# A gated mix of linear attention and a state-space convolution: moving rows by transfers, sums in plain fp32, and a reordered passage

## The chip, the cores and the metric

The kernel runs on one core of a Trainium2 chip. The metric is the device time of one execution in microseconds; lower is better. A core has five engines with a queue each: PE (TensorE, matrix products), DVE (VectorE), ACT (ScalarE), POOL (GpSimd) and SP (SyncE, which issues most transfers). Each takes its instructions in order and waits for the others through semaphores. Products are accumulated in PSUM, a memory of eight banks; all else lies in SBUF, 128 partitions wide.

## The reference

For a sequence of 2048 rows and 448 channels, two branches are mixed by a gate:

```python
g = sigmoid((x * gate_w).sum(-1, keepdims=True))
# A: linear attention, 16 heads of 28
q, k, v = split(x @ wqkv)                # heads of 28 channels
phi = lambda t: where(t > 0, t + 1, exp(t)) + 1e-6
kv  = einsum("bhsd,bhse->bhde", phi(k), v)
z   = phi(k).sum(over s)
o   = einsum("bhqd,bhde->bhqe", phi(q), kv) / (einsum("bhqd,bhd->bhq", phi(q), z) + 1e-6)
a   = o.reshape(B, S, D) @ wo
# B: each channel of x convolved with a long filter made from (log_A, A_imag, C, log_dt), plus x * D_skip
out = g * a + (1 - g) * b
```

With the inputs given here the filter of branch B is so flat that the convolution is the filter's first tap times a running sum of x. The kernel makes sure of that from the parameters (the number `okn`), and has a general convolution behind a branch that these inputs don't take.

## The kernel before

The 2048 rows are 16 pieces (`c` = 0 to 15) of 128. Matrix products are done in two or three steps on `float32r` operands: each operand is split into a high part (a cast on ScalarE) and a low part (a subtraction on VectorE or POOL), and high x high, high x low and low x high are added in PSUM. The order on each engine is the order in which the program is written; there is no scheduler.

**Main loop** (`c` = 2 to 14). Each turn does on PE: `project(c + 1, wkh, wkl, ...)`, eleven products for `k` of the next piece; one or two pairs of `do_v`, the running sum of x (a triangular matrix `tri` times `xn`); `project(c, wqh, wql, ...)`, eleven for `q`; `do_g(c)`, eleven that add phi(k)^T x into the four banks `g`. ScalarE and VectorE make phi(k) (`k_feature`, `k_high`, `k_low`; the last also adds phi(k) into `zb`, the sum of k by partition) and phi(q) (`q_post`, which writes `pq` and the gate's exponentials `e1`). POOL makes the low parts of the next pieces (`split_t`, `split_n`) and adds the running sums into `y` (`v_post`). SP loads three pieces ahead and writes the last row of each piece's running sum into row c of `u`, from which the carry between pieces comes.

`s4d_prepare` is cut into steps by `yield`; `steps(n)` runs n of them. The last computes the first tap by channel: VectorE ends with `sm` (`p0`), PE spreads it over the partitions with four transposes (`p`), and ScalarE copies it to `near`, which `v_post` needs from piece 0 on. In the loop `steps(3 if c == 4 else 1)` stands behind `q_post(c)` and ahead of `do_g(c)`, so the transposes stand between `q` and `g` of piece 4.

**The passage** (from `gate(0, NC - 1)`). The sum of k over partitions (`zo`) is taken by a matrix of ones, with `zb` split into `zh` and `zl`; it returns to `zb` on all partitions. `norm_a` multiplies `pq` by it (`prod`, POOL), `norm_b` and `norm_d` make the denominators (`den`, VectorE), `norm_c` the normalized rows (`pn`: two pieces of it on POOL, a small one on VectorE). The last `do_g` turns fill `g`, ScalarE copies it to `gs`, `kv_products(r)` multiplies it by `wv`, and `kv_split(r, ...)` masks the heads and splits (`kvh`, `kvl`). `inter` makes the carry rows `rc` from `zst`, the rows of `u` split and stacked, and the 0/1 matrix `gcat`. `mrows(j, ...)` multiplies block j of `kv` by block j of `wo`: the output matrix, four blocks of 112 rows, which replaces the weights of `k` (`mh`, `ml` = `wkh`, `wkl`). Block 3 goes to `sh`, `sl`; its rows must be moved to other partitions: 16 of them under each of blocks 0 to 2, 64 into `mh[:, 3]` and `rc`. That is done by products with the 0/1 matrix `pick`: two in each of the first three `mrows`, two in `tails()`.

**The attend loop** (`c` = 0 to 15): `turn(c + 2)` transposes `pn` (`tr`) and splits it (`th`, `tl`), `attend(c)` does eleven products `a` with the output matrix, `final_b` and `final_c` mix and send piece c - 1, `norm_c(c + 3)`, `norm_a(c + 6)`, `norm_b(c + 5)` prepare later pieces. The `q` products of piece 15 are kept as filler: `q_run(n)` does the next n of them.

Buffers matter to the order: `prod` and `pn` have two each, so a third can only be written when the reader of the first has ended.

Of the kernel before, what the change touches and what calls it, by code (L numbers as in the profile page):

```python
# [31 lines left out]
QA = (2, 2, 5)  # L32
# [7 lines left out]
KZ = 32 + NC - 1  # L40
# [129 lines left out]
def gated_mix_kernel(ctx: ExitStack, tc: tile.TileContext, xin, wq_d, wv_d, wo_d, abc_d, ldt_d, dsk_d,  # L170
                     tri_d, ident_d, mask_d, gcat_d, sel_d, pick_d, first_d, nabc_d, nldt_d, xrev_d, lag_d, out):
# [218 lines left out]
    def k_low(c):  # L390
        pk = pks.pop(c)
        pkl[c] = tp.tile([P, D], F32R, name="pkl", tag="pkl")
        for o, a, op in ((pkl[c], pkh[c].bitcast(F32), ALU.subtract), (zb, zb, ALU.add)):
            DVE.scalar_tensor_tensor(out=o, in0=pk, scalar=1e-6, in1=a, op0=ALU.add, op1=op)
# [51 lines left out]

    def z_products():
        zr = tp.tile([P, D], F32, name="zr", tag="w")[:64]
        POOL.memset(zr, 0.0)
        for o in (0, 32):  # L450
            SP.dma_start(out=zr[o:o + NC - 1], in_=u[:NC - 1])
        return zr
# [45 lines left out]
    for c in range(2, NC - 1):  # L498
        if c + 3 < NC:
            load_x(c + 3)  # L500
        if c == 2:
# [13 lines left out]
        if c + 2 < NC:
            split_t(c + 2)
        if c == NC - 2:
            zr = z_products()
            pick = xt_p.tile([P, 5, P], F32R, name="pick", tag="t")[:DJ]
            ACT.copy(pick, pickr)  # L520
# [5 lines left out]
        if c == NC - 2:
            zh = tp.tile([P, D], F32R, name="zh", tag="e")
            zl = tp.tile([P, D], F32R, name="zl", tag="t")
            ACT.copy(zh, zb)
            low(DVE, zl, zb, zh)  # L530
# [9 lines left out]
        if c == 4:  # L540
            steps(1)
            POOL.tensor_copy(gcat, gcr)
        if c + 2 < NC:
            split_n(c + 2)
# [110 lines left out]
    ACT.copy(zst, zr[:KZ])
    low(DVE, zst[32:], zr[32:KZ], zst[32:])
    zo = ps.tile([P, 512], F32, name="k", tag="k")
    do_g(NC - 2, (0, 1, 2))
    PE.matmul(zo[:1, D:D + 1], lhsT=ones[:DJ, :1], rhs=oks, start=True, stop=True)
    PE.matmul(zo[:, :D], lhsT=ones_r, rhs=zh, start=True, stop=False)  # L660
    PE.matmul(zo[:, :D], lhsT=ones_r, rhs=zl, start=False, stop=True)
    ACT.copy(zb, zo[:, :D])
# [4 lines left out]
    norm_bd(0)
    norm_a(2)
    for i in range(4):
        do_g(NC - 1, (i,))  # L670
        ACT.copy(gs[i], g[i][:, :D])
        if i == 2:
            gates_b(g2, "pkl")()
    norm_bd(1)
    norm_a(3)
    norm_c(0)
    norm_c(1)
    norm_bd(2)
    qo, q_run = pieces(NC - 1, wqh, wql, D + 2, "q")
    q_run(QA[0])  # L680
    for c in range(5):
        phi(c)
# [5 lines left out]
    def inter():  # L688
        o = ps.tile([P, 512], F32, name="z", tag="v0")
        r = tp.tile([P, D], F32R, name="rc", tag="w")  # L690
        z = tp.tile([P, D], F32R, name="zs", tag="v0")
# [1 line left out]
        PE.matmul(o[:RX, :D], lhsT=gcat, rhs=zst, start=True, stop=True)
# [4 lines left out]
    def mrows(j, pool, tag):
        o = pool.tile([P, 512], F32, name="m%d" % j, tag=tag)
        if j < 3:  # L700
            for n, w in enumerate((sh, sl)):
                PE.matmul(o[:, :D], lhsT=pick[:, j], rhs=w, start=n == 0, stop=False)
        w = woh[j]
        for n, (a, b) in enumerate(((kvh, w), (kvh, wol[j]), (kvl, w))):
            PE.matmul(o[:DJ, :D], lhsT=a[:, j], rhs=b, start=j == 3 and n == 0, stop=n == 2)  # L705
        if j < 3:
            a, b = mh[:, j], ml[:, j]
        else:
            a, b = sh, sl
        ACT.copy(a, o[:a.shape[0], :D])  # L710
        DVE.tensor_tensor(out=b, in0=o[:a.shape[0], :D], in1=a.bitcast(F32), op=ALU.subtract)

    sh = tp.tile([P, D], F32R, name="sh", tag="v0")[:DJ]
    sl = tp.tile([P, D], F32R, name="sl", tag="pkl")[:DJ]

    def tails():
        o = ps.tile([P, 512], F32, name="md", tag="v1")
        for i, w in ((3, sh), (4, sl)):
            PE.matmul(o[:, :D], lhsT=pick[:, i], rhs=w, start=i == 3, stop=i == 4)
        ACT.copy(mh[:, 3], o[:, :D])  # L720
        ACT.copy(rc[0][:DT], sh[:DT].bitcast(F32))
# [9 lines left out]
    def kv_split(r, kvp):  # L731
        m = 3 if r else 2
        DVE.tensor_tensor(out=kv[:, 2 * r:m],
                          in0=kvp[:DJ, 2 * r * DJ:m * DJ].rearrange("p (j d) -> p j d", d=DJ),
                          in1=mask[:, None, :].to_broadcast([DJ, m - 2 * r, DJ]), op=ALU.mult)
        if r:
            a, b = (w.rearrange("p (h d) -> p h d", h=4) for w in (kvp[:DJ, 3 * DJ:4 * DJ], mask))
            DVE.tensor_tensor(out=kv[:, 3, :DT].rearrange("p (h d) -> p h d", h=4), in0=a[:, :, DS:], in1=b[:, :, DS:],
                              op=ALU.mult)
# [3 lines left out]
        ACT.copy(kvh[:, rs], kv[:, rs])
# [11 lines left out]
    norm_c(2)  # L755
    q_run(QA[2])
    turn(1)
    tails()
    mrows(2, ps, "v0")
    mrows(0, p3, "a")  # L760
    mrows(1, p3, "a")
    norm_a(4)
# [65 lines left out]
def _layout(inputs):  # L828
# [41 lines left out]
    pick = np.zeros((DJ, 5, P))  # L870
    for i in range(DT):
        pick[i, 3, i] = pick[i, 4, DT + i] = 1.0
    for i in range(DJ - DT):
        pick[DT + i, i // 16, DJ + i % 16] = 1.0
# [38 lines left out]
```

## Time and profile before

| | us |
|---|---|
| median of 3 runs | 192.49 |
| the runs | 191.38, 192.49, 193.17 |
| the profiled execution, as timed | 191.0 |
| its span, first to last instruction | 189.1 |
| busy: PE, DVE, ACT, POOL | 175.4, 112.4, 96.3, 119.2 |
| mean granted TensorE clock | 0.984 |

The profile is of one execution. Its chain of waits is the work that ended last, followed back from the end; 78% of it is PE. A row of the timeline gives start, length, engine, line, operation, output and inputs with their sizes, and in brackets how long the engine had stood still and for whom. Rows that follow each other on PE overlap, since products are pipelined: the distance between starts tells what one costs. Times in the text are from the span's start.

### The profile page before, as it was taken

The numbers are of one execution on the slowest core, as the hardware profiler recorded it, in microseconds if no ns is written. First come the engines' busy times: TensorE is split into PE (matmuls) and PEld (weight loads), VectorE is DVE, ScalarE is ACT, GpSimd is POOL, SyncE is SP. The second block draws the span as 40 slices with busy tenths as digits, with TensorE's granted clock in tenths as the row PEclk, the third lists the DMA queues.
The fourth block names the chain that finished last, engine by engine and source line by source line (L and its number), as shares of the span: only waits on it lengthen the run. The fifth ranks groups of instructions, "written<-read, shape, count | busy, mean of one in ns | idle before, by whom it ended". The sixth has DMA issues, their size and how long they took to land.

```text
span 189.1 us, 2750 instructions
## 1 busy us (share of the span) xinstructions
PE 175.4 (93%) x886; PEld 154.3 (82%) x886; DVE 112.4 (59%) x238; ACT 96.3 (51%) x215; POOL 119.2 (63%) x126
## 2 busy tenths in 40 slices
PE   6999999974999999999999999998699999999980
PEld 2697798964899999999989999967599999999970
DVE  1658647745072652734625526489799999987430
ACT  3768289863062462533626644480574545564340
POOL 3359874570629697696788999367557877864000
PEclk9999999999799999999999999999999999999997
DMA  6999958900003023031233020000001212221231
GB/s 192 412 302 277 307 158 304 279 6 0 3 0 111 1 111 112 5 111 25 87 111 115 0 62 0 11 2 4 2 0 49 93 57 98 98 97 51 101 123 38
DMA packets 7771, 18.53 MB, mean 98 GB/s; under 512 B 1755, under 2 KB 4390, under 8 KB 7750
## 3 DMA queue, kind: packets, MB, share of 16 engines
q1 hardware_dynamic: 7750, 18.28, 29.1%
q8 instruction: 9, 0.15, 0.3%
q14 instruction: 12, 0.10, 0.2%
HBM read 14.50 MB, written 3.67 MB: 96 GB/s over the span
## 4 chain that ended last, share of the span: by engine, by line
PE 78%; DVE 6%; ACT 4%; POOL 4%; DMA 3%; issue 2%; SPq 1%; ACTq 0%; POOLq 0%; DVEq 0%
PE a L639 19%; PE g L425 17%; PE k L356 16%; PE q L356 15%; PE tr L617 3%; DMA xr<-in 3%; PE v L433 2%; PE v L432 2%; POOL wql L264 2%; PE m L705 1%; POOL xn L264 1%; PE v L356 1%; DVE den L565 1%; DVE pn L586 1%; POOL y L276 1%
## 5 line engine op out<-in xcount | busy, mean ns | idle before, releaser
L384 DVE SCALAR_TENSOR_TENSOR k<-k,e 128x448 f32<-128x448 f32 x14 | 8.9, 633 | 48.1 <-ACT e L383 48.1
L425 PE MATMUL g<-pkh,xn 128*128 128x448 f32 x112 | 36.4, 374 | 0.3 <-POOL xn L264 0.3
L438 POOL TENSOR_TENSOR y<-y,t 128x448 f32<-128x448 f32 x16 | 18.5, 1154 | 18.2 <-DVE t L437 18.0
L356 PE MATMUL q<-wqh,xt 128*128 128x450 f32 x120 | 28.0, 369 | 0.0
L264 POOL TENSOR_TENSOR xn<-xr,xn 128x448 fp32r<-128x448 f32 x16 | 18.5, 1154 | 14.2 <-ACT xn L274 14.2
L356 PE MATMUL k<-wkh,xt 128*128 128x448 f32 x112 | 27.1, 381 | 0.0
L639 PE MATMUL a<-wkh,th 128*128 128x448 f32 (+1 forms) x119 | 26.9, 365 | 0.0
L356 PEld LDWEIGHTS q<-wqh,xt 128*128 128x128 f32 x120 | 22.5, 189 | 2.1 <-issue 0.2
L425 PEld LDWEIGHTS g<-pkh,xn 128*128 128x128 f32 x112 | 21.4, 191 | 3.4 <-POOL xn L264 0.7
L425 PE MATMUL g<-pkl,xn 128*128 128x448 f32 x64 | 24.0, 375 | 0.0
L356 PEld LDWEIGHTS k<-wkh,xt 128*128 128x128 f32 x112 | 21.6, 194 | 2.7 <-ACT wkh L456 0.4
L382 ACT ACTIVATE e<-k 128x448 f32<-128x448 f32 x14 | 7.6, 545 | 31.7 <-PE k L356 31.7
L560 POOL TENSOR_TENSOR prod<-pq,zb 128x448 f32<-128x448 f32 x16 | 18.4, 1151 | 5.5 <-DVE den L565 4.0
L639 PEld LDWEIGHTS a<-wkh,th 128*128 128x128 f32 x119 | 20.5, 189 | 1.3
L276 POOL TENSOR_TENSOR y<-xr,rows 128x448 f32<-128x448 f32 x16 | 18.4, 1148 | 1.0 <-DMA rows<-in 1.0
L264 POOL TENSOR_TENSOR xt<-xr,xt 128x512 fp32r<-128x512 f32 x14 | 18.1, 1295 | 0.0
L583 POOL TENSOR_TENSOR pn<-pq,den 128x336 f32<-128x336 f32 x16 | 12.1, 754 | 8.9 <-PE tr L617 6.9
L621 ACT CAST th<-tr 128x512 fp32r<-128x512 f32 x16 | 9.4, 588 | 15.8 <-PE tr L617 15.5
L644 DVE SCALAR_TENSOR_TENSOR ot<-y,og,a 128x448 f32<-128x448 f32 (+1 forms) x17 | 10.5, 618 | 6.5 <-PE a L639 6.4
L639 PE MATMUL a<-wkl,th 128*128 128x448 f32 (+1 forms) x51 | 12.6, 356 | 0.0
L388 ACT ACTIVATE pkh<-k 128x448 fp32r<-128x448 f32 x14 | 7.6, 545 | 9.8 <-DVE k L384 9.8
L356 PE MATMUL q<-wql,xt 128*128 128x450 f32 x45 | 12.1, 367 | 0.4 <-POOL wql L264 0.4
(160 smaller groups left out, 338.1 us busy)
## 6 DMA issues: line engine op xcount, KB each, us to landing
xr<-in SPq DMA_DIRECT2D x15, 512.0 KB, 5.8
out<-ot SPq DMA_DIRECT2D x15, 224.0 KB, 1.9
pq<-in SPq DMA_DIRECT2D x4, 448.0 KB, 11.1
y<-in SPq DMA_DIRECT2D x2, 480.0 KB, 4.3
y<-in SPq DMA_DIRECT2D x2, 450.0 KB
wv<-in SPq DMA_DIRECT2D x1, 896.0 KB
wo<-in SPq DMA_DIRECT2D x1, 784.0 KB, 9.1
y<-in SPq DMA_DIRECT2D x1, 448.0 KB
```

The lines of the kernel that those rows point to most:

```text
L264: eng.tensor_tensor(out=o, in0=r, in1=h.bitcast(F32), op=ALU.subtract)
L276: POOL.tensor_tensor(out=y[:, c], in0=r[:, :D], in1=dsk, op=ALU.mult)
L356: PE.matmul(o[:, :n], lhsT=a, rhs=b, start=run.n == 1, stop=not seq)
L382: ACT.activation(e, pks[c], AF.Relu, scale=-1.0)
L384: DVE.scalar_tensor_tensor(out=pks[c], in0=pks[c], scalar=1.0, in1=e, op0=ALU.add, op1=ALU.max)
L425: PE.matmul(g[i][:a.shape[1], :D], lhsT=a, rhs=b, start=c == 0 and n == 0, stop=c == NC - 1 and n == len(seq) - 1)
L438: POOL.tensor_tensor(out=y[:, c], in0=y[:, c], in1=t, op=ALU.add)
L560: POOL.tensor_tensor(out=pd[c], in0=pq[:, c], in1=zb, op=ALU.mult)
L583: POOL.tensor_tensor(out=n[:, :3, :DJ].rearrange("p j (h d) -> p j h d", h=4), in0=a, in1=r[:, :H - 4].rearrange("p (j h) -> p j h", j=3)[ ...
L621: ACT.copy(h, ov)
L639: PE.matmul(a[:, lo:hi], lhsT=u_, rhs=w_[:, lo:hi], start=n == 0, stop=n == 10)
L644: DVE.scalar_tensor_tensor(out=ot[:, lo:hi], in0=y[:, c, lo:hi], scalar=og[:, c:c + 1], in1=a[:, lo:hi], op0=ALU.mult, op1=ALU.add)
```

## The change

Seven edits go together.

- The tap transposes: `steps(2 if c == 4 else 1)` and a `steps(1)` behind `project` of turn 5.
- The main loop ends with `c` = 13. Turn 14 is written out at the head of the passage, with `zo` between `q` and `g` of piece 14, the gate cut in two (pieces 0 to 13, then 14), and POOL's addition of the last running sum (`v_add`) moved to a later place. In `k_low(15)` the sum into `zb` comes first.
- The sum of k: `zb` is multiplied by `ones` as plain fp32; `zh`, `zl` and `ones_r` go.
- The carry: `u` is multiplied by `gcat` as plain fp32; `zst`, `z_products` with its two transfers, and the cast of `gcat` go.
- The rows of block 3: `pick` and its load and cast, its eight products and `tails()` go. `mrows(3)` writes high and low part side by side (`shl`), and four transfers take the rows to their partitions: three issued by SP, one by ACT. Two ScalarE copies of 64 rows do the rest. `wkh` and `wkl` become two halves of one tile `wk2`, so that one transfer serves both.
- `kv_split` is cut: the low part is now `kv_low(r)`, placed apart.
- The passage's order: `inter` ahead of the `kv` products, both of these ahead of the masks, `norm_c(0)` and `norm_c(1)` early, `norm_bd(3)` behind `turn(1)`, ten of the eleven `q` products of piece 15 in one run behind it.

```diff
-QA = (2, 2, 5)
+QA = 1
...
-        for o, a, op in ((pkl[c], pkh[c].bitcast(F32), ALU.subtract), (zb, zb, ALU.add)):
+        for o, a, op in ((pkl[c], pkh[c].bitcast(F32), ALU.subtract), (zb, zb, ALU.add))[::-1 if c == NC - 1 else 1]:
...
+        if c == 5:
+            steps(1)
...
-        steps(3 if c == 4 else 1)
-        if c < NC - 2:
-            do_g(c)
...
+        if c < 5:
+            steps(2 if c == 4 else 1)
+        do_g(c)
...
+    c = NC - 2
+    ko = project(c + 1, wkh, wkl, D, "k")
+    do_v(c + 1)
+    k_feature(c + 1, ko)
+    k_high(c + 1)
+    gate(0, c)
+    k_low(c + 1)
+    vl = v_post(c + 1)
+    qo = project(c, wqh, wql, D + 2, "q")
+    zo = ps.tile([P, 512], F32, name="zo", tag="v0")
+    PE.matmul(zo[:1, D:D + 1], lhsT=ones[:DJ, :1], rhs=oks, start=True, stop=True)
+    PE.matmul(zo[:, :D], lhsT=ones, rhs=zb, start=True, stop=True)
+    q_post(c, qo)
+    ACT.copy(zb, zo[:, :D])
+    norm_a(0)
+    norm_a(1)
+    do_g(c)
+    gate(c, c + 1)
...
+    inter()
+    q_run(QA)
     k1 = kv_products(1)
+    k0 = kv_products(0)
+    norm_bd(2)
+    norm_a(3)
     kv_split(1, k1)
-    k0 = kv_products(0)
+    kv_low(1)
     kv_split(0, k0)
-    inter()
-    q_run(QA[1])
     mrows(3, ps, "k")
+    for j, eng in ((2, SP), (0, ACT), (1, SP)):
+        eng.dma_start(out=wk2[DJ:, :, j].bitcast(F32), in_=shl[DT + 16 * j:DT + 16 * j + 16].bitcast(F32))
+    SP.dma_start(out=mh[DT:, 3].bitcast(F32), in_=shl[:DT, 1].bitcast(F32))
+    kv_low(0)
+    mrows(2, ps, "v0")
     turn(0)
+    v_add(c + 1, vl)
+    norm_c(2)
+    norm_a(4)
+    mrows(0, p3, "a")
+    ACT.copy(mh[:DT, 3], shl[:DT, 0].bitcast(F32))
+    mrows(1, p3, "a")
+    ACT.copy(rc[0][:DT], shl[:DT, 0].bitcast(F32))
+    turn(1)
     norm_bd(3)
...
```

On PE around the taps, before (`p` are the transposes, `q` and `g` those of piece 4):

```order
L356 MATMUL q<-wqh,xt 128x450 x8
L356 MATMUL q<-wql,xt 128x450 x3
L337 MATMUL p<-ident,sm 128x112 x4
L425 MATMUL g_145<-pkh,xn 128x448
L425 MATMUL g_145<-pkl,xn 128x448
```

and in the changed kernel, from the end of `g` of piece 4 (`wk_69` is the joint tile of the weights, `k` that of piece 6):

```order
L422 MATMUL g_144<-pkl,xn 128x448
L422 MATMUL g_144<-pkh,xn 128x448
L422 MATMUL g_145<-pkl,xn 64x448
L422 MATMUL g_145<-pkh,xn 128x448
L353 MATMUL k<-wk_69,xt 128x448 x11
L334 MATMUL p<-ident,sm 128x112 x4
L429 MATMUL v<-xn,tri 128x448
L430 MATMUL v<-xn,tri 128x448
```

The transposes have moved behind twenty-two products.

On ACT in the passage, before, from the cast of `kvh` (`m` is the result of `mrows`, block 3 first; `md` that of `tails`):

```order
L743 CAST kvh<-kv 112x224 x2
L694 CAST zs<-z 48x448
L710 CAST sh<-m_1366 112x448
L621 CAST th<-tr 128x512 x2
L720 CAST wkh<-md 128x448
L721 CAST rc<-sh 64x448
L710 CAST wkh<-m_1405 128x448
L710 CAST wkh<-m_1413 128x448
L710 CAST wkh<-m_1421 128x448
L625 CAST th<-rows 48x128
```

and now:

```order
L709 CAST kvh<-kv 112x224 x2
L686 CAST shl<-m_1342 112x448
L726 DMA wk_69<-shl 16x2x448
L686 CAST wk_69<-m_1353 112x448
L598 CAST th<-tr 128x512
L686 CAST wk_69<-m_1374 112x448
L735 CAST wk_69<-shl 64x448
L686 CAST wk_69<-m_1381 112x448
L737 CAST rc<-shl 64x448
L598 CAST th<-tr 128x512
L602 CAST th<-rows 48x128
```

The issue of a transfer stands among the copies, and the copy of block 2 ahead of the first `th`.

On POOL in the passage, before (`prod` is `norm_a`, `pn` is `norm_c`, `y<-y,t` the last running sum):

```order
L449 MEMSET zr 64x448
L438 TENSOR_TENSOR y<-y,t 128x448
L654 MEMSET rows 48x896
L560 TENSOR_TENSOR prod<-pq,zb 128x448 x4
L583 TENSOR_TENSOR pn<-pq,den 128x3x112
L589 TENSOR_TENSOR pn<-pq,den 128x128
L583 TENSOR_TENSOR pn<-pq,den 128x3x112
L589 TENSOR_TENSOR pn<-pq,den 128x128
L583 TENSOR_TENSOR pn<-pq,den 128x3x112
L589 TENSOR_TENSOR pn<-pq,den 128x128
L560 TENSOR_TENSOR prod<-pq,zb 128x448 x2
```

and now:

```order
L537 TENSOR_TENSOR prod<-pq,zb 128x448 x2
L648 MEMSET rows 48x896
L560 TENSOR_TENSOR pn<-pq,den 128x3x112
L566 TENSOR_TENSOR pn<-pq,den 128x128
L537 TENSOR_TENSOR prod<-pq,zb 128x448
L560 TENSOR_TENSOR pn<-pq,den 128x3x112
L566 TENSOR_TENSOR pn<-pq,den 128x128
L537 TENSOR_TENSOR prod<-pq,zb 128x448
L441 TENSOR_TENSOR y<-y,t 128x448
L560 TENSOR_TENSOR pn<-pq,den 128x3x112
L566 TENSOR_TENSOR pn<-pq,den 128x128
L537 TENSOR_TENSOR prod<-pq,zb 128x448 x2
```

The first two `pn` have moved between the `prod`, and the last running sum behind `prod` of piece 3.

More of the change, by code (lines that the diff above doesn't have):

```diff
@@ L39 @@
 RX = DT + 3 * NC
-KZ = 32 + NC - 1
 FAR = 2.0 ** 100
@@ L170, in gated_mix_kernel @@
 def gated_mix_kernel(ctx: ExitStack, tc: tile.TileContext, xin, wq_d, wv_d, wo_d, abc_d, ldt_d, dsk_d,
-                     tri_d, ident_d, mask_d, gcat_d, sel_d, pick_d, first_d, nabc_d, nldt_d, xrev_d, lag_d, out):
+                     tri_d, ident_d, mask_d, gcat_d, sel_d, first_d, nabc_d, nldt_d, xrev_d, lag_d, out):
     nc = tc.nc
@@ L187, in gated_mix_kernel @@
     const = work.enter_context(tc.tile_pool(name="const", bufs=1))
-    wkh = const.tile([P, J, D], F32R, name="wkh")
-    wkl = const.tile([P, J, D], F32R, name="wkl")
+    wk2 = const.tile([P, 2, J, D], F32R, name="wk2")
+    wkh, wkl = wk2[:, 0], wk2[:, 1]
     wqh = const.tile([P, J, D + 2], F32R, name="wqh")
@@ L196, in gated_mix_kernel @@
     mask = const.tile([DJ, DJ], F32, name="mask")
-    gcat = const.tile([KZ, RX], F32R, name="gcat")
+    gcat = const.tile([NC - 1, RX], F32, name="gcat")
     sel = const.tile([P, 1], F32, name="sel")
-    zst = const.tile([KZ, D], F32R, name="zst")
-    ones_r = const.tile([P, P], F32R, name="ones_r")
     ones = const.tile([P, P], F32, name="ones")
@@ L437, in v_post, with v_add @@
         DVE.tensor_tensor(out=t, in0=vt.pop(c)[:, :D], in1=near, op=ALU.mult)
-        POOL.tensor_tensor(out=y[:, c], in0=y[:, c], in1=t, op=ALU.add)
         if c < NC - 1:
             SP.dma_start(out=u[c:c + 1], in_=t[P - 1:P])
+            v_add(c, t)
+        return t
+    def v_add(c, t):
+        POOL.tensor_tensor(out=y[:, c], in0=y[:, c], in1=t, op=ALU.add)
     prep = s4d_prepare()
@@ L445, in steps @@
             next(prep, None)
[L447 to L452, printed above, removed]
     w = xt[0] = xt_p.tile([P, 2 * NAT], F32R, name="xt", tag="t")
@@ L492, in gated_mix_kernel @@
     DVE.memset(ones, 1.0)
-    DVE.tensor_copy(ones_r, ones)
     q_post(1, qo)
@@ L497, in gated_mix_kernel @@
     woh, wol = [], []
-    for c in range(2, NC - 1):
+    for c in range(2, NC - 2):
         if c + 3 < NC:
@@ L501, in gated_mix_kernel @@
         if c == 2:
-            gcr = tp.tile([P, D], F32, name="gcr", tag="w")[:KZ, :RX]
-            for o, i in ((mask, mask_d), (gcr, gcat_d), (sel, sel_d)):
+            for o, i in ((mask, mask_d), (gcat, gcat_d), (sel, sel_d)):
                 SP.dma_start(out=o, in_=i)
@@ L507, in gated_mix_kernel @@
             SP.dma_start(out=wo, in_=wo_d)
-        if c == NC - 3:
-            pickr = xp.tile([P, 5, P], F32, name="pickr", tag="xr")[:DJ]
-            SP.dma_start(out=pickr, in_=pick_d)
         vs = VS.get(c, ())
         ko = project(c + 1, wkh, wkl, D, "k")
+        if c == 5:
+            steps(1)
         for v in vs[:1]:
             do_v(v)
[L515 to L520, printed above, removed]
+        split_t(c + 2)
         k_feature(c + 1, ko)
@@ L525, in gated_mix_kernel @@
         k_low(c + 1)
[L526 to L530, printed above, removed]
         qo = project(c, wqh, wql, D + 2, "q")
@@ L536, in gated_mix_kernel @@
             v_post(v)
-        steps(3 if c == 4 else 1)
-        if c < NC - 2:
-            do_g(c)
[L540 to L544, printed above, removed]
+        if c < 5:
+            steps(2 if c == 4 else 1)
+        do_g(c)
+        split_n(c + 2)
         for j in {11: (0, 1), 12: (2, 3)}.get(c, ()):
@@ L650, in final_c @@
             ACT.copy(pq[:, c, lo:hi], a[:, lo:hi])
-    gate(0, NC - 1)
+    c = NC - 2
[16 more added lines that the diff above has]
+    gate(c, c + 1)
     g2 = gates_a(1, NC - 1)
     POOL.memset(rows[DT:RX, :2 * D], 0.0)
[L655 to L662, printed above, removed]
+    last = gates_b(g2, "pkl")
     DVE.tensor_copy(okn, zo[:1, D:D + 1])
-    norm_a(0)
-    norm_a(1)
-    do_g(NC - 2, (3,))
     norm_bd(0)
+    norm_c(0)
+    last()
     norm_a(2)
+    norm_bd(1)
+    norm_c(1)
     for i in range(4):
-        do_g(NC - 1, (i,))
+        do_g(c + 1, (i,))
         ACT.copy(gs[i], g[i][:, :D])
[L672 to L682, printed above, removed]
+    qo, q_run = pieces(c + 1, wqh, wql, D + 2, "q")
+    for i in range(5):
+        phi(i)
     gps.close()
@@ L692, in inter @@
         rc.append(r)
-        PE.matmul(o[:RX, :D], lhsT=gcat, rhs=zst, start=True, stop=True)
+        PE.matmul(o[:RX, :D], lhsT=gcat, rhs=u[:NC - 1], start=True, stop=True)
         ACT.copy(z[DT:RX], o[DT:RX, :D])
@@ L696, in inter @@
                                  in1=o[DT:RX, :D], op0=ALU.mult, op1=ALU.add)
+    shl = xn_p.tile([P, NX], F32R, name="shl", tag="n")[:DJ, :2 * D].rearrange("p (i d) -> p i d", i=2)
     def mrows(j, pool, tag):
         o = pool.tile([P, 512], F32, name="m%d" % j, tag=tag)
-        if j < 3:
-            for n, w in enumerate((sh, sl)):
-                PE.matmul(o[:, :D], lhsT=pick[:, j], rhs=w, start=n == 0, stop=False)
         w = woh[j]
         for n, (a, b) in enumerate(((kvh, w), (kvh, wol[j]), (kvl, w))):
[L705 to L721, printed above, removed]
+            PE.matmul(o[:DJ, :D], lhsT=a[:, j], rhs=b, start=n == 0, stop=n == 2)
+        a, b = (mh[:DJ, j], ml[:DJ, j]) if j < 3 else (shl[:, 0], shl[:, 1])
+        ACT.copy(a, o[:DJ, :D])
+        DVE.tensor_tensor(out=b, in0=o[:DJ, :D], in1=a.bitcast(F32), op=ALU.subtract)
     def kv_products(r):
@@ L743, in kv_split, with kv_low @@
         ACT.copy(kvh[:, rs], kv[:, rs])
+    def kv_low(r):
+        rs = slice(2 * r, 2 * r + 2)
         low(DVE, kvl[:, rs], kv[:, rs], kvh[:, rs])
+    inter()
+    q_run(QA)
     k1 = kv_products(1)
+    k0 = kv_products(0)
+    norm_bd(2)
+    norm_a(3)
     kv_split(1, k1)
-    k0 = kv_products(0)
+    kv_low(1)
     kv_split(0, k0)
-    inter()
-    q_run(QA[1])
     mrows(3, ps, "k")
-    turn(0)
-    norm_bd(3)
[L755 to L762, printed above, removed]
+    for j, eng in ((2, SP), (0, ACT), (1, SP)):
[3 more added lines that the diff above has]
+    mrows(2, ps, "v0")
+    turn(0)
+    v_add(c + 1, vl)
[6 more added lines that the diff above has]
+    turn(1)
+    norm_bd(3)
     norm_a(5)
@@ L865, in _layout @@
     k = np.arange(NC)[None, :] - np.arange(NC)[:, None]
-    gcat = np.zeros((KZ, RX))
-    gcat[:NC - 1, DT:] = gcat[32:, DT:] = np.repeat(k[:-1] > 0, 3, axis=1)
+    gcat = np.zeros((NC - 1, RX))
+    gcat[:, DT:] = np.repeat(k[:-1] > 0, 3, axis=1)
     sel = np.zeros((P, 1))
     sel[DT:RX, 0] = -1.0 * (np.arange(RX - DT) % 3 == 1)
[L870 to L874, printed above, removed]
     h = np.arange(DJ) // DH
@@ L889, in _layout @@
         f(sel),
-        f(pick),
         first,
```

## The prediction

> **What bounds the kernel now.** I read the busy shares first, then PE's waits, then the chain of waits. The first fence has PE's row of the busy shares and the longest rows of PE's waits (who waited for whom: us in total, times, longest).
>
> ```profile
> PE 175.4 (93%) x886; PEld 154.3 (82%) x886; DVE 112.4 (59%) x238; ACT 96.3 (51%) x215; POOL 119.2 (63%) x126
> ...
> PE p L337 <- DVE sm L303: 3.7, 1, 3.7
> ...
> PE m L705 <- ACT kvh L743: 1.5, 1, 1.5
> PE k L728 <- ACT gs L671: 0.6, 1, 0.6
> ```
>
> TensorE is the bound, so the change is worth what it takes from PE's work and from PE's waits. The largest wait is one: the tap transposes `p` wait 3.7 us for VectorE. The chain of waits (start us, us, what) shows what surrounds it, the windows below it the granted clock (after the five engines come the clock, then the DMA share and GB/s), and the timeline two operations of ScalarE.
>
> ```profile
> 39.27 0.55 ACT e L382
> 39.85 0.59 ACT e L383
> ...
> 41.70 0.62 DVE pkl L394
> ...
> 44.96 0.17 DVE sm L303
> ...
> 45.18 0.60 PE p L337 x4
> 45.77 3.27 PE g L425 x11
> 49.05 2.76 PE k L356 x11
> 51.81 0.21 PE v L432
> ...
> 54.90 2.27 PE g L425 x11
> 57.16 2.25 PE k L356 x11
> ...
> 40.00:50.00 10.00, 6.30 (x27) 5.28 (x26) 3.97 (x19) 3.04 (x7) 5.29 (x6) 0.83 0.00 1
> 50.00:60.00 10.00, 10.00 (x50) 9.13 (x49) 3.77 (x7) 3.80 (x8) 4.44 (x5) 1.00 0.11 35
> ...
> 45.81 0.53 ACT L338 COPY rows<-p 128x448 f32<-128x448 f32 x1 [3.64 <-PE p L337]
> 46.76 0.62 ACT L268 CAST xt<-xr 128x512 fp32r<-128x512 f32 x1
> ```
>
> The reader is to see two losses. PE stands still from 45.18 - 3.7 = 41.48 to 45.18. Then the same eleven `g` products take 3.27 where they take 2.27 an iteration later, and `k` 2.76 for 2.25: the clock granted over 40 to 50 us is 0.83, and 1.00 in the next window.
>
> **Part 1: the tap transposes one iteration later.** They move behind `g` of piece 4 and `k` of piece 6. Before, 41.48 to 51.81, where the first `v` starts, is 10.33 us. After, the same work is 2.27 (`g`) + 2.25 (`k`) + 0.44 (four transposes, the `tr` row of the next fence) = 4.96. That is a gain of 5.37, of which 1.51 is the clock (3.27 - 2.27 + 2.76 - 2.25).
>
> Is the cover there? `p` would start at 41.48 + 4.52 = 46.0; its input `sm` ends at 44.96 + 0.17 = 45.13 and follows from nothing that PE does after 41.48. Next to be late is `k` of piece 7, due at 46.0 + 0.44 + 2.25 + 2.27 + 0.82 (two `v` pairs) = 51.8. It needs its PSUM bank, and ScalarE now copies the taps ahead of that work: transposes done 46.5, copy 0.53, cast of `xt` 0.62, two exponentials 0.55 and 0.59 = 48.8, then four VectorE passes at about 0.62 (the `pkl` row) = 51.3. Half a microsecond is left, so I charge nothing. SP's queue keeps its order there. The POOL cast of `gcat` and the VectorE cast of `ones_r` go, neither waited for by PE.
>
> **Part 2: PE's work in the passage.** The passage runs from `k` of the last piece to the second `a`. The fence has chain rows, then timeline rows of PE.
>
> ```profile
> 116.71 2.24 PE k L356 x11
> ...
> 123.55 0.41 PE k L660
> 123.95 0.47 PE k L661
> ...
> 134.00 0.90 PE m L705 x3
> ...
> 141.43 2.25 PE a L639 x11
> 143.69 0.44 PE tr L617 x4
> 144.13 2.26 PE a L639 x11
> ...
> 129.79 1.74 PE L728 MATMUL tr<-gs,wv 128*112 128x112 f32 x16
> 131.46 0.46 PE L693 MATMUL z<-zst,gcat 47*112 47x448 f32 x1
> ...
> 137.38 0.36 PE L702 MATMUL m<-sh,pick 112*128 112x448 f32 x1
> ...
> 137.79 0.57 PE L705 MATMUL m<-wo,kvh 112*112 112x448 f32 x2
> ```
>
> The eight `pick` products go: two of them run from 137.38 to 137.79, so 8 x 0.205 = 1.64 us less. The sums become plain fp32. No 448-column fp32 product is in the trace; the nearest are the eight 112-column ones (16 records) from 129.79 to 131.46, 0.209 each, four times that for 448 columns: 0.84. The lower end is the split product's own 0.205, the upper 1.74/8 x 4 = 0.87. I take 0.84: `zo` costs 0.84 for 0.41 + 0.47, `z` 0.84 for 0.46. PE's work falls by 1.64 + 0.04 - 0.38 = 1.30 at face value. Counted out, the new passage up to the second `a` holds 23.4 us of PE work: `k`, `v`, `q` 4.90, `zo` 0.96 with the small product, two `g` and `o` 4.64, `z` 0.84, `q` 2.25, `kv` 3.34, four `m` 2.44, four `tr` 1.76, the first `a` 2.25. Before, the stretch lasted 144.13 - 116.71 = 27.42. So 4.04 us is the most the passage can give.
>
> **Part 3: the waits of the new passage.** I reckon on the old clock, each engine in its new order, with these durations (timeline, the waits' causes in brackets; DMA rows: KB each, us to landing).
>
> ```profile
> 125.33 1.00 DVE L411 TENSOR_SCALAR og<-og 128x15 f32<-128x15 f32 x1
> 128.09 0.62 DVE L565 TENSOR_REDUCE den<-prod 128x16 f32<-128x448 f32 x1
> 132.41 0.47 DVE L570 SCALAR_TENSOR_TENSOR den<-den,e 128x16 f32<-128x16 f32 x1
> 162.44 0.14 DVE L779 TENSOR_SCALAR og<-og 128x1 f32<-128x1 f32 x1
> ...
> 125.14 2.26 POOL L560 TENSOR_TENSOR prod<-pq,zb 128x448 f32<-128x448 f32 x2 [1.55 <-ACT zb L662]
> 132.10 0.75 POOL L583 TENSOR_TENSOR pn<-pq,den 128x336 f32<-128x336 f32 x1
> 132.81 0.40 POOL L589 TENSOR_TENSOR pn<-pq,den 128x128 f32<-128x128 f32 x1
> 161.64 1.15 POOL L560 TENSOR_TENSOR prod<-pq,zb 128x448 f32<-128x448 f32 x1
> ...
> 129.40 3.59 SPq L597 DMA_DIRECT2D rows<-phs  x5
> ...
> out<-ot SPq DMA_DIRECT2D x2, 112.0 KB, 2.1
> pq<-in SPq DMA_DIRECT2D x4, 448.0 KB, 11.1
> ```
>
> VectorE and POOL hinder each other: two small VectorE operations last until a POOL operation ends, L570 until L583 does (132.10 + 0.75 = 132.85, and 132.41 + 0.47 = 132.88), L411 until the first `prod` does (125.14 + 1.13 = 126.27, and 126.33).
>
> - `zo` must wait for the last sum into `zb`, which stands behind the three gate operations: `k` ends at 118.95, two exponentials, one VectorE pass, the gate (0.5) and the pass into `zb` make 122.0, and PE is there at 121.6: 0.4.
> - The old 1.5 before `m` (kvh) shrinks. PE ends the `kv` products at 116.71 + 4.90 + 0.4 + 0.96 + 4.64 + 0.84 + 0.2 + 3.34 = 132.0. VectorE has the denominators of piece 2 just ahead of the masks; their second operation, L570, waits for `prod` 3 on POOL. POOL starts the first `prod` near 123.7, behind `zo` and a copy of 0.53, and runs without a gap through `prod` 0 and 1, a memset, `pn` 0, `prod` 2, `pn` 1 and `prod` 3 to about 131.2. From L570's end to `m` it was 134.00 - 132.88 = 1.1: 132.3. PE waits 0.3. The 0.6 before `kv` is covered by `z` and one `q`.
> - After the first `m` (132.3 to 132.9) ScalarE copies its rows into `shl` behind the second `kvh` cast, 133.9, and VectorE makes their low part, 134.5. Only then comes `kvl` for block 0, whose inputs both lie in SBUF like L570's; it runs into POOL's `pn` 2, which starts after `tr` 0 near 134.1, so it ends at 134.1 + 0.75 + 0.35 (half a pass) = 135.2. PE wants it at 134.35: 0.9.
> - The new wait is at `tr` of piece 3. ScalarE issues one row transfer, and that issue waits for `shl` low at 134.5 with everything behind it waiting too; SP's issues take 3.59/5 = 0.72, so 135.2 (bounds: nothing and 1.4, twice as much). Behind it stand seven ScalarE copies of 0.53 to 0.62, to 139.05; then VectorE's low part and `den` 3 (0.6 each), 140.3; POOL's `prod` 5 (1.15), which reuses the buffer that `den` 3 reads and stands ahead of `pn` 3 (0.75 + 0.40): 142.6. PE reaches that `tr` at 132.9 + 0.61 + 0.44 + 1.5 + 0.6 + 0.44 + 2.05 + 0.44 + 2.25 = 141.2 (`m`, `tr`, `m` with its 0.9, `m`, `tr`, ten `q` products, `tr`, `a`). It waits 1.4. The next `tr` comes out 0.2 late in the same way, behind `prod` 6.
>
> Sum of waits 0.4 + 0.3 + 0.9 + 1.4 + 0.2 = 3.2; 4.04 - 3.2 leaves a gain of 0.8. The row transfers are not in it: SP issues three by 134.5 + 3 x 0.72 = 136.7, landing takes 2.1 (the 112 KB row), 138.8, and the seventh product of the first `a`, at 139.0 + 6 x 0.205 = 140.2, is the first that reads the last. The cover is 1.4 us.
>
> **Sum.** 5.4 + 0.8 = 6.2. The profiled execution took 191.0 (span 189.1 and 1.9 around it), giving 184.8; the runs' median is 192.49, 1.5 above it, and I state the forecast against the median: 192.5 - 6.2 = 186.3.
>
> **The rivals.**
>
> - The passage's waits vanish, because POOL and VectorE fall in step and the ScalarE issue is short. For it: three of the four waits hang on queue order within half a microsecond. Against: the POOL-VectorE row L570. It gives up to 3.5 in place of 0.8: 183.6.
> - The passage loses: `pn` stays late for several pieces, since VectorE and POOL keep each other waiting there too, and each wait doubles; nothing but that every copy on ScalarE stands in one line speaks for it. 4.04 - 6.4 is a loss of 2.4, of which I count 2: 192.5 - 5.4 + 2.0 = 189.1.
> - The one-column gate of piece 14, now between the products on POOL, is held as L411 was. It would end with the second `prod` near 126.1, where PE wants it at 125.2: 0.9 more, 187.2. Against it: L779, of one column, took 0.14 in the midst of POOL's `prod` (161.64 + 1.15). The Trainium skill (SBUF — State Buffer, section "Who interferes with whom") says that `tensor_scalar` can take the pair of ports shared with GpSimd and that the one that comes second is blocked outright. By that rule, if one column counts, this rival holds; the trace agrees for L411's fifteen columns and not for L779's one.
> - The change does not do what it says at the taps: the stall goes to `k` of piece 7, with clock and all. Only 0.5 us of cover speaks for it; a full 5.4 would have to be lost there again: 191.7.
> - Slower than before: the row transfers land late. Every microsecond past the cover is PE's, so it needs a landing of 2.1 + 1.4 + 6.2 = 9.7 us to reach the old time, and 1.9 more to be seen. The `pq` row shows 11.1, but for 448 KB at the start with the DMA engines full. At 12 it gives 192.5 + 12 - 9.7 = 194.8.
>
> **How the numbers follow.** Forecast 0.55; no waits 0.15; the passage loses 0.15; the gate held 0.07; the stall moves 0.05; late transfers 0.03. The range 183.6 to 189.1 takes the first four, 0.92, less what the spread of the runs (191.38 to 193.17) pushes out of it. Beyond 1% (1.9 us, about what a measurement of this kernel tells from no change): faster 0.92, same 0.05, slower 0.03.
>
> **What would show it.** Right: no PE wait at `p`, the granted clock at 1.00 between 40 and 50 us, `v` of piece 0 starting near 46.4; two records of about 0.4 for `zo` and for `z`; a PE wait of 1 to 2 us at `tr` with POOL's `pn` as its cause; none at the first `a`. Wrong: a PE wait at `k` of piece 7; a first `a` that waits for a DMA; a `g` after `zo` waiting for the gate; further waits at the later `tr`.

## The result, and the profile after

| | before | after |
|---|---|---|
| median of the runs, us | 192.83 (4 runs, 191.38 to 193.33) | 185.72 (4 runs, 185.38 to 186.15) |
| ratio, 95% interval | | 0.964 [0.959, 0.970] |
| the profiled execution, us | 191.0 | 185.38 |
| its span, us | 189.1 | 183.6 |
| mean granted clock | 0.984 | 0.998 |

The forecast was 186.3 us, the time is 185.72. The gain is 7.1 us by the medians and 5.6 by the two profiled executions; experiment 4 takes up the difference between these two numbers. Three runs beside the experiments count as slow and are left out of all that follows: two of before (193.78 and 193.80 us) and one of experiment 6 (440.35 us).

The first fence has PE's row of the busy shares of after, the second those of PE's waits in it that the change bears on (who waited for whom: us in total, times, longest). Line numbers are those of the changed kernel from here on.

```profile
PE 173.2 (94%) x879; PEld 151.4 (82%) x879; DVE 112.9 (62%) x238; ACT 94.7 (52%) x212; POOL 118.8 (65%) x124
```

```profile
PE m L684 <- DVE kvl L261: 0.7, 1, 0.7
PE p L334 <- DVE sm L300: 0.6, 1, 0.6
PE m L684 <- ACT kvh L709: 0.6, 1, 0.6
PE zo L640 <- DVE zb L391: 0.4, 1, 0.4
...
PE tr L594 <- POOL pn L560: 0.3, 1, 0.3
```

Of the 5.5 us that the span is shorter, 2.2 are PE's busy time (175.4 to 173.2), in which the slow clock counts too; the rest is time in which PE stood still. The 3.7 at `p` are 0.6 now, and the four other waits stand where the forecast put waits of the new passage. The next fence shows the taps: rows of the chain of waits of after (start us, us, what). The one behind it is the row of its windows for 40 to 50 us (length; busy time of PE, PEld, DVE, ACT, POOL; granted clock; DMA share; GB/s).

```profile
46.31 0.17 DVE sm L300
46.53 0.60 PE p L334 x4
47.12 0.22 PE v L429
...
50.23 2.22 PE g L422 x11
52.45 2.24 PE k L353 x11
```

```profile
40.00:50.00 10.00, 9.36 (x49) 8.29 (x48) 5.66 (x21) 4.03 (x10) 5.69 (x5) 1.00 0.01 2
```

The reader is to see that `g` and `k` behind the transposes take 2.22 and 2.24 (3.27 and 2.76 before), that the clock is 1.00 there, and that the first `v` starts at 47.12 instead of 51.81: 4.69 us earlier. `k` of piece 7 starts at 52.45, just where `g` ends (50.23 + 2.22), so the stall has not moved there.

For the passage the same instructions are compared in the two timelines, the first two rows from before, the last two from after.

```profile
116.55 1.79 PE L356 MATMUL k<-wkh,xt 128*128 128x448 f32 x8
...
146.57 1.68 PE L639 MATMUL a<-wkh,th 128*128 128x448 f32 x7
...
111.82 2.40 PE L353 MATMUL k<-wk,xt 128*128 128x448 f32 x11
...
141.04 1.68 PE L616 MATMUL a<-wk,th 128*128 128x448 f32 x7
```

`k` of the last piece starts 4.73 us earlier than before (111.82 against 116.55), the second `a` 5.73 (138.15 against 143.88), the third 5.53 (141.04 against 146.57). So the passage gives 1.0 by the second `a`, and 0.2 of it is lost again at the next transposes: 0.8 net.

### The profile page after: what moved, and what is told of

The parts are those of the page before. It is cut to its first block, busy times and chain, and to the rows that moved or that the text cites. A ratio compares the mean times of both kernels' runs of the same rounds, so it can differ in the third digit from the quotient of the medians.

```text
span 183.6 us, 2736 instructions
## 1 busy us (share of the span) xinstructions
PE 173.2 (94%) x879; PEld 151.4 (82%) x879; DVE 112.9 (62%) x238; ACT 94.7 (52%) x212; POOL 118.8 (65%) x124
## 4 chain that ended last, share of the span: by engine, by line
PE 71%; DVE 9%; POOL 6%; issue 6%; ACT 5%; ACTq 0%; POOLq 0%; DVEq 0%
PE a L616 19%; PE k L353 15%; PE q L353 14%; PE g L422 12%; PE tr L594 3%; PE q L279 3%; PE v L430 2%; PE v L429 2%; POOL wql L261 2%; POOL y L273 2%; POOL xn L261 1%; DVE den L542 1%; PE v L353 1%; DVE den L547 1%; POOL prod L537 1%
## 5 line engine op out<-in xcount | busy, mean ns | idle before, releaser
L616 PE MATMUL a<-wk,th 128*128 128x448 f32 (+1 forms) x170 | 39.0, 362 | 0.0
L353 PE MATMUL k<-wk,xt 128*128 128x448 f32 x154 | 34.8, 370 | 0.0
L353 PEld LDWEIGHTS k<-wk,xt 128*128 128x128 f32 x154 | 28.8, 188 | 3.7 <-ACT wk L450 0.6
L616 PEld LDWEIGHTS a<-wk,th 128*128 128x128 f32 x170 | 29.8, 189 | 2.0
L422 PE MATMUL g<-pkl,xn 128*128 128x448 f32 x64 | 23.4, 366 | 0.0
L422 PEld LDWEIGHTS g<-pkl,xn 128*128 128x128 f32 x64 | 11.2, 175 | 1.2 <-issue 0.2
```

The source lines that it names most:

```text
L353: PE.matmul(o[:, :n], lhsT=a, rhs=b, start=run.n == 1, stop=not seq)
L422: PE.matmul(g[i][:a.shape[1], :D], lhsT=a, rhs=b, start=c == 0 and n == 0, stop=c == NC - 1 and n == len(seq) - 1)
L616: PE.matmul(a[:, lo:hi], lhsT=u_, rhs=w_[:, lo:hi], start=n == 0, stop=n == 10)
```

## The experiments

All were timed against the kernel before. Before's median was 192.25 us beside experiments 1 to 4 (12 runs) and 191.97 beside 5 to 8 (10 runs). Within each group of four the kernels ran on the same chip.

### 1. The taps alone

The kernel before, with only the tap transposes moved:

```diff
+        if c == 5:
+            steps(1)
...
-        steps(3 if c == 4 else 1)
+        if c < 5:
+            steps(2 if c == 4 else 1)
```

> The kernel before with the tap transposes behind g of piece 4 and k of piece 6, and nothing else of the change. Theory (two gains that add up): the first v starts 4.7 us earlier than before, as in the changed kernel (51.81 to 47.12), and the whole is 4.5 to 5 us shorter than the kernel before, with PE's wait at p 0.6 us. Rival (the passage's new order is what gives the time, or the stall returns at k of piece 7): under 2 us.

Measured: 186.79 us (185.97 to 187.75), ratio 0.972 [0.966, 0.978], so 5.5 us below before by the medians and 5.0 by the profiled executions (186.03). PE's waits of this kernel, as above, with the line numbers of the kernel before:

```profile
PE m L707 <- ACT kvh L745: 1.5, 1, 1.5
...
PE k L730 <- ACT gs L673: 0.6, 1, 0.6
PE p L337 <- DVE sm L303: 0.5, 1, 0.5
```

The old waits of the passage are back (1.5 and 0.6), the 3.7 at `p` are 0.5. The larger part of the gain is this one edit. Two of the four runs took 187.54 and 187.75 us, both at a mean clock of 0.987; they have no trace, so what slowed them stays open.

### 2. The passage alone

The changed kernel with the transposes put back where they were:

```diff
-        if c == 5:
-            steps(1)
...
-            steps(2 if c == 4 else 1)
+            steps(3 if c == 4 else 1)
```

> The changed kernel with the tap transposes back between q and g of piece 4. Theory: the stall of 3.7 us and the low clock return, and only the passage's gain is left, 0.8 us against the kernel before (from k of the last piece to the third a). Rival (the passage gives nothing by itself): no difference from the kernel before; second rival (the passage gives most): 3 us or more.

Measured: 191.47 us (190.18 to 191.83, 10 runs), ratio 0.9954 [0.9918, 0.9991], so 0.8 us below before. From the waits of this kernel, and from its chain:

```profile
PE p L334 <- DVE sm L300: 4.1, 1, 4.1
```

```profile
47.53 3.44 PE g L422 x11
```

The stall and the slow clock behind it are back (`g` takes 3.44). All the rest of the change, six of the seven edits with eight products less and four transfers, is worth 0.8 us by the medians, 0.2 to 1.6 by the interval. How this divides among the six was tried for the sum of k alone (experiment 8). The profiled execution, 191.74 us, is no faster than before's 191.0: the stall is 4.1 in it, and an early `k` waits 0.7 that before doesn't have. The passage itself shows the gain: from `q` of piece 13 to the third `a`, by the chains, this kernel takes 33.81 us (113.63 to 147.44), before 34.58 (112.24 to 146.82). The two parts add up to 6.3 (5.5 + 0.8); the median of after, timed apart from this group, is 6.5 below this group's median of before, within the intervals.

### 3. The low part of piece 6 later

`p` still waits 0.64 in after, where the forecast had no wait. The timeline of after (start, length, engine, line, operation, output and inputs, in brackets the idle time and its releaser) shows VectorE's scale of `pq` held:

```profile
42.70 1.15 POOL L261 TENSOR_TENSOR xn<-xr,xn 128x448 fp32r<-128x448 f32 x1 [0.71 <-ACT xn L271]
42.73 1.37 DVE L369 TENSOR_SCALAR t<-e 128x448 f32<-128x448 f32 x1
```

Before, the same scale took 0.38:

```profile
42.78 0.38 DVE L372 TENSOR_SCALAR t<-e 128x448 f32<-128x448 f32 x1
```

The tap copy used to hold back ScalarE's cast of `xn`; now the cast is early, POOL's low part of `xn` follows at once and meets the scale, 0.03 us ahead of it. To test this, the split of piece 6 was put one iteration later, where nothing of the taps is left to be held:

```diff
+        if c == 5:
+            split_n(6)
...
-        split_n(c + 2)
+        if c != 4:
+            split_n(c + 2)
```

> The changed kernel with the split of xn of piece 6 issued one turn later, behind k of piece 6. In the changed kernel ScalarE casts xn 6 early, since the copy of the taps no longer stands ahead of it, POOL's low part runs from 42.70 to 43.85, and VectorE's L369 takes 1.37 us in place of 0.38. Theory (POOL's operation holds VectorE's): L369 takes 0.4 us, sm ends 1.0 to 1.3 us earlier, p does not wait, and the span is 0.6 us shorter than the changed kernel's. Rival (VectorE is late there for another reason): L369 stays over 1 us and p waits 0.6 us as before.

Measured: 184.72 us (184.58 to 185.16), ratio 0.959 [0.956, 0.963]. PE has no wait at `p`, and the scale is free, as a row of this kernel's timeline shows, then rows of its chain:

```profile
43.14 0.38 DVE L369 TENSOR_SCALAR t<-e 128x448 f32<-128x448 f32 x1
```

```profile
41.84 2.22 PE g L422 x11
44.05 2.24 PE k L353 x11
46.30 0.38 PE p L334 x4
46.68 0.22 PE v L429
```

From the start of `g` to `v` it is 4.84 us, against 4.96 forecast. The missing 0.7 us at the taps was POOL's operation. The span, 183.4 us, is only 0.2 shorter than after's and not 0.6 as expected, because this execution came to `g` of piece 4 later (41.67 against 41.27 in the timelines); from there to the third `a` it takes 98.95 us (to 140.62), after 99.77 (to 141.04).

### 4. The clock without the wait's place

The kernel before, with 17 products whose result nobody reads ahead of the transposes. PE then works where it waited, but the transposes stay as late as they were:

```diff
+        f = ps.tile([P, 512], F32, name="f", tag="v0")
+        for i in range(17):
+            PE.matmul(f[:, :D], lhsT=wkh[:, 1, :P], rhs=wkh[:, 2], start=True, stop=True)
```

> The kernel before with 17 products of 448 columns, whose result nobody reads, ahead of the tap transposes, so that TensorE works while it waits for VectorE. Theory (the clock falls because TensorE stands still): the granted clock stays at 1.00 between 40 and 50 us, g takes 2.3 us and k 2.25, and the kernel is 1.5 us shorter than before although the transposes start no earlier. Rival (the clock falls for another reason, or the stall is all there is): g still takes 3.3 us and the time is that of the kernel before.

Measured: 189.81 us (189.34 to 190.75), ratio 0.988 [0.983, 0.992]. The chain of this kernel from the transposes on:

```profile
44.85 0.60 PE p L340 x4
45.44 2.28 PE g L428 x11
47.72 2.25 PE k L359 x11
49.97 0.21 PE v L435
```

`g` takes 2.28 and `k` 2.25. From the start of `p` to the first `v` it is 5.12 us (44.85 to 49.97), where before took 6.63 (45.18 to 51.81): 1.51 less, just what the forecast put down to the clock. `p` starts 0.33 earlier only because this execution was ahead before the taps (the exponential that starts at 39.27 in before starts at 38.95), so the profiled executions differ by 1.7 (191.0 to 189.34). By the medians the gain is 2.4. So the loss to the clock seems larger in a usual run of before than in the one that was profiled. Only that one has a trace, but the mean clocks fit. Of before's 22 runs beside the experiments, the six with a mean clock of 0.984 or more took 190.65 to 191.82 us, the seven with 0.976 or less 192.16 to 193.54. Its profiled execution, with 0.984 and 191.0, belongs to the first. The runs of after lie between 0.991 and 0.998.

### 5. SP issues all four row transfers

The stall at `tr` of piece 3 was said to begin with the transfer that ScalarE issues. After's timeline has that issue, as long as taken (0.71, 0.72 forecast), and the transposes that wait:

```profile
130.42 1.44 SPq L726 DMA_DIRECT2D wk<-shl  x2
130.43 0.71 ACTq L726 DMA_DIRECT2D wk<-shl  x1
...
131.91 0.59 SPq L727 DMA_DIRECT2D wk<-shl  x1
...
134.92 1.67 PE L616 MATMUL a<-wk,th 128*128 128x448 f32 x7
...
137.71 0.69 PE L594 MATMUL tr<-ident,pn 128*128 128x128 f32 x4 [0.31 <-POOL pn L560]
```

```diff
-    for j, eng in ((2, SP), (0, ACT), (1, SP)):
+    for j, eng in ((2, SP), (0, SP), (1, SP)):
```

> After's kernel with the fourth row transfer issued by SyncE instead of ScalarE; nothing else moves. Theory: ScalarE's issue of 0.71 us at 130.43 is the first link of the chain that ends in the normalised piece 3, so without it the wait of PE for that piece (0.31 in the waits of after, about 0.5 by the start of its transposes) shrinks to 0.0 to 0.2. The chain shortens by less than 0.71: the copy of block 0's product waits for PE then, which leaves 0.44 of it, and VectorE's own low parts end at 134.16, which leaves 0.33. So 0.2 to 0.4 us below after: 185.3 to 185.5, span about 183.3. SyncE's fourth issue then starts near 132.6 and lands near 135.1, ahead of its first reader at 136.1, so that the first product of a shows no wait. Rival: piece 3 is held by GpSimd's own order (the product of piece 5 ahead of it) and nothing moves: wait still 0.3 and 185.7. Second rival: the later issue makes the first a wait, 0.5 us or more, 186.2.

Measured: 185.25 us (184.99 to 185.30), ratio 0.964 [0.960, 0.969]; 0.33 below after by the profiled executions (185.05), 0.47 by the medians, though those come from different chips. The two rows in the timeline of this kernel:

```profile
135.05 1.67 PE L616 MATMUL a<-wk,th 128*128 128x448 f32 x7
...
137.41 0.69 PE L594 MATMUL tr<-ident,pn 128*128 128x128 f32 x4
```

From the first `a` to the transposes it is 2.36 us, against 2.79 in after: 0.43 less. Of this 0.08 goes again at the next transposes; from `q` of piece 13 to the third `a`, by the chains, this kernel takes 33.42 us (107.58 to 141.00) and after 33.77 (107.52 to 141.29). The issue was the head of that chain, and the transfers are still in time.

### 6. Edits 3 and 5 together

> After's kernel with two edits together: the split of piece 6's natural form put behind the taps' last scale, and the fourth row transfer issued by SyncE. Theory: the two gains lie in different places (42 to 47 us and 130 to 138 us) and add: 184.7 for the first alone, less 0.2 to 0.4, so 184.3 to 184.5, with neither the wait of PE for the gates' product of the taps nor the one for piece 3. Rival: the second is worth nothing, 184.7.

Measured: 184.44 us (184.07 to 184.52, 5 runs), ratio 0.960 [0.955, 0.965]. It is 0.81 below experiment 5 on the same chip, which prices edit 3 by itself. This kernel beats both that were given: it is 0.88 us below after by the profiled executions (184.50), 1.28 by the medians, though those come from different chips. Of the waits in the first fence, those at `p` and at `tr` are gone:

```profile
PE m L687 <- DVE kvl L261: 0.7, 1, 0.7
PE m L687 <- ACT kvh L712: 0.6, 1, 0.6
PE zo L643 <- DVE zb L391: 0.4, 1, 0.4
```

### 7. Late transfers

```diff
-    for j, eng in ((2, SP), (0, ACT), (1, SP)):
+    for j, eng in ((2, SP), (2, SP), (0, ACT), (1, SP)):
```

> After's kernel with the transfer of block 2's rows issued twice by SyncE, the second one writing the same values to the same place. This leaves the results as they are and makes the rest of SyncE's transfers later: the second has to wait until the first has landed, 3.4 us from its issue at 130.42, so block 2's rows are there near 137.2, block 1's and the low rows of the fourth near 137.9. Theory of the prediction: the transfers had a cover of about 1.4 us behind the first product of a (134.92) and no more, so PE now waits 2.3 to 3.0 us there, and the time grows by 1.9 to 3.0 us, since the later wait for piece 3 is covered by it: 187.6 to 188.7. Rival: the stretch behind it is held by VectorE and GpSimd anyway and half of the wait comes back: 186.7. Second rival: the second transfer does not wait for the first, everything is 0.7 us later and inside the cover: 185.7, no wait.

Measured: 185.57 us (185.27 to 186.40), ratio 0.967 [0.962, 0.972]. The time is that of the second rival, but not for its reason: SP did hold the second transfer back until the first had landed, as its row of the waits shows, and its three issues take 3.69 us where two took 1.44. The row of the waits comes first, then rows from the timeline of this kernel, then its transfers (KB each, median us to landing):

```profile
SPq L726 <- DMA wk<-shl: 1.6, 1, 1.6
```

```profile
130.52 3.69 SPq L726 DMA_DIRECT2D wk<-shl  x3
...
134.27 0.58 SPq L727 DMA_DIRECT2D wk<-shl  x1
...
135.31 0.31 PEld L616 LDWEIGHTS a<-wk,th 128*128 128x128 f32 x2 [0.26 <-DVE th L599]
135.34 1.89 PE L616 MATMUL a<-wk,th 128*128 128x448 f32 x7
135.94 0.91 PEld L616 LDWEIGHTS a<-wk,th 128*128 128x128 f32 x5 [0.32 <-ACT th L598]
...
137.89 0.61 PE L594 MATMUL tr<-ident,pn 128*128 128x128 f32 x4
```

```profile
wk<-shl SPq DMA_DIRECT2D x3, 56.0 KB, 2.3
```

The second transfer of block 2 was issued at 132.95 and landed 2.3 us after that, at 135.25. In after the only one was issued at 130.42, took 3.4 and landed at 133.82. So SP's last issue is 2.4 us later (134.27 against 131.91), but the landing of block 2 only 1.4, where I had reckoned with 3.4. The first `a` waits just 0.26 and 0.32. The trace names VectorE and ScalarE there, with operations on later pieces that the first `a` doesn't read. I put these waits down to the transfers, because the times fit: the first product reads block 2, and its weights are loaded at 135.31, just behind 135.25; the third reads block 1, which was issued at 133.63 and would land at 135.93 if it too takes 2.3, and its weights are loaded at 135.94. The time doesn't show these waits: from `q` of piece 13 to the third `a` this kernel takes 33.82 us (107.58 to 141.40), 0.05 more than after, because the wait for piece 3 that stood behind is gone, spent ahead of time. So a landing 1.4 us later costs nothing here. From which delay on it costs its full length wasn't tried.

### 8. The sum of k as two fp32r products

After's kernel with the sum split again, `ones_r` being `ones` as fp32r:

```diff
+    zh = tp.tile([P, D], F32R, name="zh", tag="v0")
+    zl = tp.tile([P, D], F32R, name="zl", tag="w")
+    ACT.copy(zh, zb)
+    low(DVE, zl, zb, zh)
...
-    PE.matmul(zo[:, :D], lhsT=ones, rhs=zb, start=True, stop=True)
+    PE.matmul(zo[:, :D], lhsT=ones_r, rhs=zh, start=True, stop=False)
+    PE.matmul(zo[:, :D], lhsT=ones_r, rhs=zl, start=False, stop=True)
```

> After's kernel with the carry's total computed as before the change: the sum is split in a high part (ScalarE copy) and a low part (VectorE), and two fp32r products replace the one fp32 product, at the same place in TensorE's order. Theory: TensorE gains about 0.6 of work (two records of 0.51 become two of 0.2), but the split stands on the path between the sum (ready at 117.4) and the product, ScalarE 0.54 and VectorE 0.62 of it, so the wait of TensorE there grows from 0.4 to about 1.6: the time is 0.4 to 0.8 us longer than after, 186.1 to 186.5. Rival: the split is covered by other work and the shorter product wins: 185.2, with a wait of at most 0.6.

Measured: 186.00 us (185.77 to 186.25), ratio 0.969 [0.964, 0.973]. After's row, then the two of this kernel:

```profile
117.44 1.02 PE L640 MATMUL zo<-zb,ones 128*128 128x448 f32 x2 [0.43 <-DVE zb L391]
```

```profile
117.76 0.47 PE L646 MATMUL zo<-zh,ones_r 128*128 128x448 f32 x1 [1.07 <-ACT zh L640]
118.42 0.47 PE L647 MATMUL zo<-zl,ones_r 128*128 128x448 f32 x1 [0.19 <-DVE zl L262]
```

The wait of 0.43 becomes 1.07 + 0.19 (about 1.6 was expected), with products that take half as long together. Between `q` of piece 13 and the third `a`, by the chains, this kernel takes 34.50 us (107.21 to 141.71) and after 33.77 (107.52 to 141.29): 0.73 more. By the medians it is 0.3 above after and 0.4 above experiment 7, which ran on the same chip. The plain fp32 product pays although it costs PE more, because it takes two operations off the path. Put back into this order, the old form costs nearly all that the passage gives by the trace, and about half of it by the medians.

## Why the prediction was right, step by step

**Part 1, the taps (5.37).** 4.69 by the trace. The order, the cover of `k` of piece 7 and the clock came out as said. The step that failed is "`sm` ends at 45.13 and follows from nothing that PE does after 41.48": true of PE, but `sm` also follows from POOL, which the tap copy had kept away from VectorE as long as it stood ahead of the cast of `xn`. That is the 0.64 at `p`; experiment 3 takes it away and comes to 4.84.

**Part 2, PE's work (1.30 less).** The eight `pick` products went as priced. The fp32 products were taken at 0.84: `zo` fills PE from 117.44 to the first `g`, which by the second one's start (118.50 - 0.205) is 118.30, so 0.86; `z` runs from 122.97 to the next product at 123.90, 0.93, above the upper end of 0.87 that I had set. Between `k` of the last piece and the second `a` PE needs 26.33 - 2.55 of waits = 23.8 us, where I counted 23.4: besides `z`, some 0.1 each at the ten `q` products and where PE restarts after a wait.

**Part 3, the waits (3.2).** By the start times in after's timeline they are 0.5 at `zo`, 0.65 at the first `m`, 0.9 at the `m` of block 0 (two products behind the first, which starts at 129.78, its last would have started near 130.25, and starts at 131.16), 0.5 at `tr` of piece 3 and 0.2 at the next: 2.75. Each stands where it was put, with the cause it was given.

```profile
128.10 0.66 PE L684 MATMUL m<-wo,kvh 112*112 112x448 f32 x2 [0.58 <-ACT kvh L709]
...
131.16 0.46 PE L684 MATMUL m<-wo,kvl 112*112 112x448 f32 x1 [0.73 <-DVE kvl L261]
...
137.61 0.40 POOL L566 TENSOR_TENSOR pn<-pq,den 128x128 f32<-128x128 f32 x1
```

The mis-sized term is the wait at `tr` of piece 3, 0.5 for 1.4. Its chain was right: `pn` 3 was forecast for 142.6 on the old clock and ended at 137.61 + 0.40 + 4.73 = 142.74. That the end fits so well is in part luck: ScalarE's issue ended 0.67 us later than forecast (130.43 + 0.71 + 4.73 = 135.87 for 135.2), and the seven copies behind it took 0.57 less (3.28 for 3.85). PE, with 0.45 more wait and some 0.3 more work ahead of it, came about 0.75 later than forecast, so most of the wait was spent before it began. The two errors, waits 0.45 too high and work 0.4 too low, cancel because the end of the stretch hangs on that chain and not on PE, and the passage came out at the 0.8 forecast, in the trace and in experiment 2.

**The sum and the median.** Against its own profiled execution the forecast was 184.8, and 185.38 came: 0.6 too good, the taps' shortfall. Against the median it was 186.3, and 185.72 came: 0.6 too cautious. I had carried the 1.5 us between before's profiled execution and its median over to after unchanged. Experiment 4 and the clocks of the runs speak for it that much of it was the clock behind the stall, which goes with the stall; after's median is 0.3 above its profiled execution. That the median was missed by only 0.6 is therefore in part luck: 0.7 too much at the taps stood against 1.15 of spread that the forecast had carried over.

**The rivals.** That the waits vanish: no, all five are there, though experiment 5 shows that the one at `tr` of piece 3 could go. That the passage loses: no, experiment 2. The held gate: it stands in the midst of POOL's two products, as the rival wanted, and took 0.14:

```profile
119.10 1.15 POOL L537 TENSOR_TENSOR prod<-pq,zb 128x448 f32<-128x448 f32 x1 [5.84 <-ACT zb L642]
...
119.39 0.14 DVE L406 TENSOR_SCALAR e<-e 128x1 f32<-128x1 f32 x1
```

The rule of the Trainium skill (SBUF — State Buffer, section "Who interferes with whom") holds for the 448-column scale that experiment 3 sets free, 1.37 for 0.38, and not for one column. The stall did not move to `k` of piece 7. The transfers were in time: the first `a` has no wait at 134.92, and in experiment 7 block 2's rows landed 1.4 us later at no cost.

## What to carry to other kernels

A wait of the bounding engine is priced with what follows it: 3.7 us of standing still cost another 1.5 in clock by the trace, 2.4 by the medians, and filling it with idle work already gained that part. When an operation is moved away from an engine's queue, ask what it kept back there: here a copy on ScalarE had kept POOL off VectorE, at 0.6 us. Where a stretch ends on a chain of other engines, as here, a small error in when the bounding engine arrives changes the wait behind it by the same amount and leaves the end alone, so the sum over the stretch is better known than each of its waits.

## What the runs showed of the hardware that was not expected

- The spread of a kernel's runs can be its clock: 22 runs of before went from 190.65 to 193.54 us with mean clocks from 0.989 down to 0.971, while four runs with the wait filled (experiment 4) spread over 1.4 us at 0.989 to 0.997. The two slower runs of experiment 1 show that the stall isn't all of it, and a mean clock also counts the end of the span, where PE has nearly finished (0.76 from 183 us on in before). The Trainium skill (TensorE: Matmul & The Clock Gate, Part 1) says that about 3.4 us of idleness bring the array to half rate, judged by a free-running window. The trace agrees: the clock is 0.67 and 0.66 from 45 to 50 us, behind waits of 3.7 (before) and 4.1 (experiment 2), and stays at 1.00 from 50 to 170 us in the profiled execution of experiment 1, which has a wait of 1.5 there. A free-running window would also explain that before's loss differs from run to run; no run here shows the window itself.
- A transfer to a place that an earlier transfer still writes to held SP's queue until that one had landed: SP waited 1.6 us for it, at a semaphore event of the program that after doesn't have (experiment 7).
- A plain fp32 product of 448 columns took 0.86 and 0.93 us in two records, against 0.205 for an fp32r one.
